# Transposing queries and keys by DMA instead of on TensorE, in a windowed attention fused with a gated feed-forward layer

## The chip, the cores and the metric

One core of a Trainium2 chip runs the whole program. The metric is device time in microseconds (us) from one launch; lower is better. Shown are the median of three runs and one profiled execution, from which all durations come.

## What is computed

Eight heads of attention over four sequences, each with 768 positions and head dimension 64. A query sees the first 8 keys and the last 96; a bias falls with the distance. The result, 3072 rows of 512, goes through a feed-forward layer that multiplies a relu branch with a linear one.

```python
scores = scale * np.matmul(q, k.transpose(0, 1, 3, 2))
is_global = pos[None, :] < int(n_global)          # n_global = 8
is_local = (rel >= 0) & (rel < int(n_local))      # n_local = 96
scores = scores + bias[None, :, :, :]             # bias = -slope * distance
scores = np.where(keep, scores, -1000000000.0)
a = np.exp(scores - np.max(scores, axis=-1, keepdims=True))
a = a / (np.sum(a, axis=-1, keepdims=True) + 1e-09)
x = (a @ v), laid out as (4 * 768, 8 * 64)
out = (np.maximum(x @ w_gate, 0.0) * (x @ w_val)) @ w_out   # 512 -> 1536 -> 512
```

Inputs and output are float32; the matmuls run in bf16 with float32 sums.

## The kernel before

The work is cut into eight halves: half s is the first or second 384 positions of sequence s // 2, with all heads. Position 3p + n of a half lies on partition p, so a half's queries are three blocks of 128, numbered n. Heads go in four pairs p.

Attention of one half, for each pair (`attention_pieces`):

- `piece_cast` (C, GpSimd from half 1 on): casts queries and keys of two heads to bf16 (L224).
- `piece_t` (T): six TensorE transposes of 128 x 128 into one PSUM tile `tp` (L235). VectorE copies the two heads' queries into a zero-padded tile `qp` (L240, L241), so that one matmul gives the scores of both. ScalarE (L252 or L259) and VectorE (two copies) put the keys into `kT` in the order of positions: seven tiles j of 8 global and 120 other keys. The second half of a sequence fills up tile 3 and writes tiles 4 to 6.
- `piece_qk` (QK, three groups): scores (L276), exponential on ScalarE (L279), times a mask in bf16 on VectorE (L288). Two PSUM buffers.
- `piece_av` (AV, one per head): values times weights (L304). The values carry columns of ones, so the sums come along; ScalarE takes their logarithm (`lnd`, L313) and the exponential of its negative (`rcp`, L318), and VectorE scales into `xT` (L321). Two PSUM buffers.

The feed-forward layer of half c (`ffn_pieces`) is 12 pairs of a gate piece (L346, relu on ScalarE L349) and a value piece (L356, product on VectorE L358), then six output pieces; each second one is copied by ScalarE (`osb`, L370) and stored by SP (L371).

Each engine works in the order in which the code issues its instructions (`manual_schedule`); semaphores hold it where an input is missing. `weave` sets that order: it issues feed-forward pieces, and between them the attention items, spread evenly by the pieces' weights. From c = 2 on, pass c weaves the layer of half c with the attention of half c+1. Before that the last eight gate/value pieces of halves 0 and 1 and both output layers are woven with the attention of half 2. SP issues the loads of q and k (`load_qk`), the spreading of global values and the stores; GpSimd issues the loads of v and of the weights.

## Time and profile before

| | |
|---|---|
| runs | 305.38, 305.5, 304.17 us; median 305.38 |
| profiled execution | 305.4 us, span 303.3 us |
| mean granted TensorE clock | 0.954 |
| TensorE matmuls busy | 254.7 us, 84% of the span |
| ScalarE, VectorE, GpSimd busy | 170.0, 163.9, 70.0 us |
| transposes (L235) | 192 matmuls, 17.2 us busy |
| GpSimd casts (L224) | 59, 30.4 us busy |
| bytes moved by DMA | 27.51 MB |

Busy times of matmuls overlap, since they are pipelined; what a matmul costs TensorE is read from one start to the next. The span is from the first to the last instruction. In rows of the profile PE is TensorE, DVE VectorE, ACT ScalarE, POOL GpSimd, SP SyncE; a bracket at a row's end gives the idle time before it and what ended it.

### The profile page before, as it was taken

How to read it: one execution, taken by the hardware profiler on the slowest of the kernel's cores; microseconds unless marked ns; L12 is line 12 of the kernel's file. 1: busy time of each engine (PE TensorE's matmuls, PEld its weight loads, DVE VectorE, ACT ScalarE, POOL GpSimd, SP SyncE). 2: the span in 40 equal slices, each digit the busy share in tenths (PEclk: the TensorE clock that was granted, in tenths of full speed). 3: DMA queues.
4: the chain of work that ended last, by engine and by line, in shares of the span. 5: the costliest groups of instructions: out<-in, count | busy, mean ns of one | idle time of the engine just before them, and what ended most of it. 6: DMA issues, size and time to landing. Idle time of an engine off the chain costs nothing.

```text
span 303.3 us, 4823 instructions
## 1 busy us (share of the span) xinstructions
PE 254.7 (84%) x1680; PEld 149.7 (49%) x1680; DVE 163.9 (54%) x458; ACT 170.0 (56%) x357; POOL 70.0 (23%) x134
## 2 busy tenths in 40 slices
PE   1264787549999889989998989999998899899994
PEld 0132345324555445655565546554664466545551
DVE  7655346552446545764476637763567457643420
ACT  8356326462345674767465755676576647664321
POOL 8960159200812400340226000400030000000000
PEclk9997589776999999999999999999999999999999
DMA  7999955908970724442862418001700110001002
GB/s 194 178 200 198 223 168 35 72 2 236 211 50 1 104 89 147 129 28 43 110 202 13 56 60 240 0 2 71 241 4 0 69 37 1 2 35 70 2 6 98
DMA packets 52400, 27.51 MB, mean 91 GB/s; under 512 B 28120, under 2 KB 49112, under 8 KB 52376
## 3 DMA queue, kind: packets, MB, share of 16 engines
q0 software_dynamic: 31856, 7.91, 26.2%
q1 hardware_dynamic: 20520, 19.30, 20.7%
q8 instruction: 13, 0.21, 0.3%
q14 instruction: 11, 0.09, 0.1%
HBM read 28.38 MB, written 6.29 MB: 114 GB/s over the span
## 4 chain that ended last, share of the span: by engine, by line
PE 68%; ACT 14%; DVE 14%; issue 2%; ACTq 0%
PE ff_ps L356 19%; PE ff_ps L346 19%; PE ff_ps L365 18%; DVE xT L321 6%; PE av_ps L304 5%; PE qk_ps L276 5%; ACT lnd L313 4%; ACT rcp L318 3%; ACT es L279 2%; PE tp L235 2%; DVE qp L241 2%; ACT grelu L349 2%; ACT kT L252 1%; DVE qp L240 1%; DVE ht L358 1%
## 5 line engine op out<-in xcount | busy, mean ns | idle before, releaser
L346 PE MATMUL ff_ps<-xT,wg 128*128 128x384 bf16 x384 | 82.3, 338 | 6.1 <-DVE ht L358 3.4
L356 PE MATMUL ff_ps<-xT,wv 128*128 128x384 bf16 x384 | 81.6, 337 | 2.6 <-ACT grelu L349 2.6
L358 DVE TENSOR_TENSOR ht<-ff_ps,grelu 128x384 bf16<-128x384 f32 x96 | 53.0, 554 | 40.1 <-PE ff_ps L356 36.5
L349 ACT ACTIVATE grelu<-ff_ps 128x384 bf16<-128x384 f32 x96 | 47.4, 493 | 39.4 <-DVE ht L358 22.8
L365 PE MATMUL ff_ps<-wo_sb,ht 128*128 128x512 bf16 x288 | 68.1, 379 | 0.0
L321 DVE TENSOR_TENSOR xT<-av_ps,rcp 64x384 bf16<-64x384 f32 x64 | 35.5, 555 | 46.1 <-ACT rcp L318 38.9
L279 ACT ACTIVATE es<-qk_ps 128x432 bf16<-128x432 f32 (+2 forms) x96 | 48.8, 537 | 8.8 <-PE qk_ps L276 8.1
L356 PEld LDWEIGHTS <-wv 128*128 128x128 bf16 x384 | 37.4, 100 | 31.0 <-issue 11.7
L346 PEld LDWEIGHTS <-wg 128*128 128x128 bf16 x384 | 37.4, 101 | 28.6 <-issue 8.0
L288 DVE TENSOR_TENSOR es<-es,m_all 128x432 bf16<-128x432 bf16 (+6 forms) x144 | 41.2, 320 | 18.8 <-ACT es L279 17.6
L276 PE MATMUL qk_ps<-qp,kT 128*128 128x432 bf16 (+6 forms) x144 | 33.3, 305 | 18.7 <-ACT es L279 9.1
L224 POOL CAST qk<-qs 128x384 bf16<-128x384 f32 x28 | 14.3, 511 | 131.3 <-DMA qs<-in_q_dram 96.5
L365 PEld LDWEIGHTS <-ht 128*128 128x128 bf16 x288 | 27.0, 97 | 26.9
L313 ACT ACTIVATE lnd<-av_ps 64x384 f32<-64x384 f32 x64 | 31.1, 486 | 14.2 <-PE av_ps L304 12.5
L304 PE MATMUL av_ps<-es,vbuf 128*128 128x216 bf16 (+5 forms) x288 | 29.6, 239 | 9.7 <-DVE xT L321 9.2
L304 PEld LDWEIGHTS <-vbuf 128*128 128x128 bf16 x288 | 24.2, 104 | 25.3 <-issue 16.9
L128 POOL DMA_DIRECT2D vbuf<-in_v_dram x28 | 24.4, 876 | 11.2 <-PE av_ps L304 11.2
L276 PEld LDWEIGHTS <-kT 128*128 128x128 bf16 x144 | 14.1, 101 | 25.6 <-issue 10.2
L370 ACT COPY osb<-ff_ps 128x512 f32<-128x512 f32 x24 | 14.1, 587 | 20.7 <-PE ff_ps L365 20.4
L235 PE MATMUL tp<-ident,qk 128*128 128x128 bf16 x192 | 17.2, 230 | 7.5 <-DVE qk L224 6.1
L235 PEld LDWEIGHTS <-qk 128*128 128x128 bf16 x192 | 13.7, 103 | 11.7 <-DVE qk L224 6.1
L224 POOL CAST qk<-ks 128x384 bf16<-128x384 f32 x31 | 16.1, 522 | 14.4 <-DMA ks<-in_k_dram 14.4
(50 smaller groups left out, 102.0 us busy)
## 6 DMA issues: line engine op xcount, KB each, us to landing
out_dram<-osb SPq DMA_DIRECT2D x24, 256.0 KB, 2.0
qs<-in_q_dram SPq DMA_DIRECT2D x6, 768.0 KB, 5.9
ks<-in_k_dram SPq DMA_DIRECT2D x6, 768.0 KB, 8.1
vbuf<-in_v_dram POOLq DMA_DIRECT2D x24, 120.0 KB, 4.4
qs<-in_q_dram SPq DMA_DIRECT2D x8, 192.0 KB, 9.2
ks<-in_k_dram SPq DMA_DIRECT2D x8, 192.0 KB, 4.5
wg<-in_moe_w_gate_dram POOLq DMA_DIRECT2D x3, 512.0 KB, 8.1
wv<-in_moe_w_val_dram POOLq DMA_DIRECT2D x3, 512.0 KB, 9.9
```

Of the source, the lines that this page charges most:

```text
L235: nc.tensor.matmul(tp[:, i, n * 128 : (n + 1) * 128], lhsT=qk[:, i, n], rhs=ident, is_transpose=True, start=(i == 0 and n == 0), stop=(i = ...
L276: nc.tensor.matmul(ps[:, c : c + n_], lhsT=kt[:, j, :], rhs=qd[:, :, :, a : a + w], start=True, stop=True)
L279: nc.scalar.activation(es[:, 0:cols], ps[:, 0:cols], AF.Exp, bias=0.0, scale=scale)
L288: nc.vector.tensor_mul(e4, e4, mk)
L304: nc.tensor.matmul(av3[:, :, a : a + w], lhsT=vb[:, j, z0 : z0 + 128], rhs=es[:, c : c + NN * w].rearrange("k (n p) -> k n p", n=NN), star ...
L313: nc.scalar.activation(ln[o0 : o0 + 64], av[d0 : d0 + 64, 0:QH], AF.Ln, bias=0.0, scale=1.0)
L321: nc.vector.tensor_tensor(xT_of[s][r, p, :], av_of[s, p, e_][r, 0:QH], rc[r], op=ALU.mult)
L346: nc.tensor.matmul(psg[:, 0:QH], lhsT=w_of(wg, dc, fc), rhs=xT[:, dc, :], start=(dc == 0), stop=(dc == N_DC - 1))
L349: nc.scalar.activation(gr, psg[:, 0:QH], AF.Relu, bias=0.0, scale=1.0)
L356: nc.tensor.matmul(psv[:, 0:QH], lhsT=w_of(wv, dc, fc), rhs=xT[:, dc, :], start=(dc == 0), stop=(dc == N_DC - 1))
L358: nc.vector.tensor_tensor(ht[:, fc, :], psv[:, 0:QH], st["gr"], op=ALU.mult)
L365: nc.tensor.matmul(ps2, lhsT=ht[:, fc, n * 128 : (n + 1) * 128], rhs=wo_sb[:, fc, :], start=(fc == 0), stop=(fc == N_FC - 1))
```

## The change

Halves 0 and 1 are as before. From half 2 on TensorE transposes nothing. GpSimd casts queries to `qz`, where each head's 64 columns stand in a block of 128 whose other half is zero, and keys to `kc`. SP issues six DMA transposes per half: for each n, eight blocks of 128 x 128 from `qz` to `qT`, and four from `kc` to `kN`. The transposed zeros give the padding of `qT`. GpSimd then copies keys from `kN` into `kT` in the order of positions. These early pieces of half c+2 are woven into pass c behind the first nine attention items, a half ahead of use. For halves 2 and 3 they stand elsewhere: half 2's between the last gate/value pieces of halves 0 and 1, half 3's behind the attention of half 2, which is now woven with the output pieces alone. To make room, six pools lose a buffer.

```diff
-    stage = ctx.enter_context(tc.tile_pool(name="stage", bufs=3))
-    cast_pool = ctx.enter_context(tc.tile_pool(name="cast", bufs=4))
-    es_pool = ctx.enter_context(tc.tile_pool(name="es", bufs=4))
-    rc_pool = ctx.enter_context(tc.tile_pool(name="rc", bufs=3))
+    stage = ctx.enter_context(tc.tile_pool(name="stage", bufs=2))
+    cast_pool = ctx.enter_context(tc.tile_pool(name="cast", bufs=3))
+    es_pool = ctx.enter_context(tc.tile_pool(name="es", bufs=3))
+    rc_pool = ctx.enter_context(tc.tile_pool(name="rc", bufs=2))
...
-    osb_pool = ctx.enter_context(tc.tile_pool(name="osb", bufs=3))
+    osb_pool = ctx.enter_context(tc.tile_pool(name="osb", bufs=2))
...
-    qp = [const.tile([128, 2, QH], BF16, name=f"qp{i}") for i in range(4)]
+    qTb = [const.tile([128, HP, 2, QH], BF16, name=f"qT{i}") for i in range(2)]
+    kNb = [const.tile([128, HP, QH], BF16, name=f"kN{i}") for i in range(2)]
+    qz = [const.tile([128, NN, HP, 2, 128], BF16, name=f"qz{i}") for i in range(2)]
+    kc = [const.tile([128, NN, DM], BF16, name=f"kc{i}") for i in range(2)]
...
+    def put_keys(copy, copy_small, kt, src, half):
...
+        if half == 0:
+            copy(*put(0, 3, 0, NG, 128))
+            copy_small(*put(3, 4, 120, NG, NG + 24))
+            copy_small(kt[:, :, 0:NG], kt[:, 0:1, NG : 2 * NG].to_broadcast([128, NT, NG]))
+        else:
+            copy(*put(4, 6, 32, NG, 128))
+            copy_small(*put(3, 4, 0, NG + 24, 128))
+            copy_small(*put(6, 7, 112, NG, NG + 48))
...
+    def piece_cast_all(s, p):
+
+        qsrc = qs_of[s][:, 2 * p : 2 * p + 2, :].rearrange("t e (n d) -> t e n d", n=NN)
+        for e in range(2):
+            nc.gpsimd.tensor_copy(qz[s % 2][:, :, p, e, 64 * e : 64 * e + 64], qsrc[:, e])
+        nc.gpsimd.tensor_copy(
+            kc[s % 2].rearrange("t n (h d) -> t h n d", d=D)[:, 2 * p : 2 * p + 2],
+            ks_of[s][:, 2 * p : 2 * p + 2, :].rearrange("t e (n d) -> t e n d", n=NN))
+
+    def piece_x(s, n):
+        nc.sync.dma_start_transpose(
+            out=qTb[s % 2].rearrange("d p e t -> d (p e) t")[:, :, n * 128 : (n + 1) * 128],
+            in_=qz[s % 2][:, n].rearrange("t p e z -> t (p e z)"))
+        nc.sync.dma_start_transpose(
+            out=kNb[s % 2][:, :, n * 128 : (n + 1) * 128], in_=kc[s % 2][:, n])
+
+    def piece_order(s, p):
+        b, half = divmod(s, 2)
+        put_keys(nc.gpsimd.tensor_copy, nc.gpsimd.tensor_copy, kT[b % 2][p], kNb[s % 2][:, p], half)
+
+    def early_pieces(s):
+        out = [(0.0, lambda p=p: piece_cast_all(s, p)) for p in range(HP)]
+        out += [(0.0, lambda n=n: piece_x(s, n)) for n in range(NN)]
+        out += [(0.0, lambda p=p: piece_order(s, p)) for p in range(HP)]
+        return out
...
+        if s >= 2:
+            return QK(0) + QK(1) + AV(0) + QK(2) + AV(1) + QK(3) + AV(2) + AV(3)
...
-    weave(f1_0[2 * G2 :] + f1_1[2 * G2 :] + f2_0 + f2_1, attention_pieces(2), 0.2)
+    weave(f1_0[2 * G2 :] + f1_1[2 * G2 :], early_pieces(2))
+    weave(f2_0 + f2_1, attention_pieces(2) + early_pieces(3))
 
     for c in range(2, NHALF):
+        early = []
         if c + 2 < NHALF:
             load_qk(c + 2, 0, H)
             load_v_half(c + 2)
+            early = early_pieces(c + 2)
         f1, f2 = ffn_pieces(c)
-        weave(f1 + f2, attention_pieces(c + 1) if c + 1 < NHALF else [])
+        a_ = attention_pieces(c + 1) if c + 1 < NHALF else []
+        items = []
+        for i in range(max(len(a_), len(early))):
+            items += a_[i : i + 1]
+            if i >= 8:
+                items += early[i - 8 : i - 7]
+        items += early[max(0, len(a_) - 8):] if len(early) > len(a_) - 8 else []
+        weave(f1 + f2, items)
```

Three places show what stands where on an engine. On VectorE before, in pass 3 (attention of half 4), from the scaling of pair 0's result to the second mask of pair 2; `qp3` and `kT0_3` are the query and key tiles of pair 3:

```order
L321 TENSOR_TENSOR xT_1915<-av_ps_1895,rcp_1916 64x384
L321 TENSOR_TENSOR xT_1915<-av_ps_1909,rcp_1916 64x384
L358 TENSOR_TENSOR ht_1708<-ff_ps_1920,grelu_1907 128x384
L240 COPY qp3_114<-tp_1926 64x384
L241 COPY qp3_114<-tp_1926 64x384
L254 COPY kT0_3_106<-tp_1926 128x24
L255 COPY kT0_3_106<-kT0_3_106 128x7x8
L358 TENSOR_TENSOR ht_1708<-ff_ps_1945,grelu_1943 128x384
L288 TENSOR_TENSOR es0_1952<-es0_1952,m_all_122 128x432
L288 TENSOR_TENSOR es1_1964<-es1_1964,m_all_122 128x432
```

And now, on VectorE in the same pass, from the scaling of pair 0's result past the second mask of pair 2:

```order
L348 TENSOR_TENSOR xT_1792<-av_ps_1773,rcp_1793 64x384
L348 TENSOR_TENSOR xT_1792<-av_ps_1786,rcp_1793 64x384
L315 TENSOR_TENSOR es0_1805<-es0_1805,m_all_126 128x432
L387 TENSOR_TENSOR ht_1692<-ff_ps_1809,grelu_1802 128x384
L315 TENSOR_TENSOR es1_1826<-es1_1826,m_all_126 128x432
L387 TENSOR_TENSOR ht_1692<-ff_ps_1830,grelu_1823 128x384
L387 TENSOR_TENSOR ht_1692<-ff_ps_1846,grelu_1841 128x384
```

The four copies are gone, and feed-forward products stand between the masks of one pair. On SP before, from the loads of half 3 to those of half 4, six stores follow one another:

```order
L107 DMA qs_869<-in_q_dram 128x8x192
L107 DMA ks_870<-in_k_dram 128x8x192
L371 DMA out_0_dram<-osb_1058 128x512
L371 DMA out_0_dram<-osb_1098 128x512
L371 DMA out_0_dram<-osb_1147 128x512
L371 DMA out_0_dram<-osb_1192 128x512
L371 DMA out_0_dram<-osb_1237 128x512
L371 DMA out_0_dram<-osb_1270 128x512
L107 DMA qs_1273<-in_q_dram 128x8x192
L107 DMA ks_1274<-in_k_dram 128x8x192
```

Now, on SP from the third of these stores to the loads of half 4 (`qT1`, `kN1`, `qz1`, `kc1` are half 3's tiles):

```order
L400 DMA out_0_dram<-osb_1160 128x512
L400 DMA out_0_dram<-osb_1222 128x512
L276 DMA_TRANSPOSE qT1_112<-qz1_116 128x8x128
L279 DMA_TRANSPOSE kN1_114<-kc1_118 128x4x128
L276 DMA_TRANSPOSE qT1_112<-qz1_116 128x8x128
L279 DMA_TRANSPOSE kN1_114<-kc1_118 128x4x128
L400 DMA out_0_dram<-osb_1254 128x512
L276 DMA_TRANSPOSE qT1_112<-qz1_116 128x8x128
L279 DMA_TRANSPOSE kN1_114<-kc1_118 128x4x128
L400 DMA out_0_dram<-osb_1284 128x512
L110 DMA qs_1287<-in_q_dram 128x8x192
L110 DMA ks_1288<-in_k_dram 128x8x192
```

Half 3's transposes stand behind the fourth store, its last two behind the fifth. On GpSimd now, from the last casts of half 2 to the first of half 3, the key copies stand between and wait for the transposes:

```order
L270 CAST qz0_115<-qs_767 128x3x64 x2
L271 CAST kc0_117<-ks_768 128x2x3x64
L242 COPY kT1_0_107<-kN0_113 128x3x120
L243 COPY kT1_0_107<-kN0_113 128x24
L244 COPY kT1_0_107<-kT1_0_107 128x7x8
L242 COPY kT1_1_108<-kN0_113 128x3x120
L243 COPY kT1_1_108<-kN0_113 128x24
L244 COPY kT1_1_108<-kT1_1_108 128x7x8
```

Before, casts of the next half and value loads followed casts there, with no copies between.

More of the change, by code (lines that the diff above doesn't have):

```diff
@@ L204 @@
         nc.vector.memset(kT[0][p][:, 3, 32:128], 0.0)
-    for i in range(2):
-        nc.scalar.copy(qp[i][64:128, 0, :], zeros[64:128])
-        nc.scalar.copy(qp[i][0:64, 1, :], zeros[0:64])
+    for p in range(2):
+        nc.scalar.copy(qTb[0][64:128, p, 0, :], zeros[64:128])
+        nc.scalar.copy(qTb[0][0:64, p, 1, :], zeros[0:64])
     for h in range(H):
@@ L250, in piece_t @@
[L250 to L263 removed]
+        put_keys(nc.scalar.copy, nc.vector.tensor_copy, kt, tp[:, 1, :], half)
@@ L395, in weave, with zero_q @@
             f()
+    def zero_q(i, p):
+        nc.gpsimd.memset(qTb[i][64:128, p, 0, :].bitcast(mybir.dt.uint32), 0)
+        nc.gpsimd.memset(qTb[i][0:64, p, 1, :].bitcast(mybir.dt.uint32), 0)
     a0 = attention_pieces(0)
@@ L420 @@
     load_v_half(1)
+    for p in range(HP):
+        zero_q(1, p)
     load_w_group(2)
@@ L433 @@
         fill(nc.gpsimd, 1, j)
+    for i in range(2):
+        nc.gpsimd.memset(qz[i].rearrange("t n p e z -> t (n p e z)").bitcast(mybir.dt.uint32), 0)
     load_qk_after(2)
```

36 lines of the change are left out of this document (10 added, 26 removed).

## The prediction

> **What bounds the kernel now.** I read the head of the profile page first, then the same by stage, then TensorE in order of time through one pass, then the waits over five passes, and at the end the transfers.
>
> The page, from which the span, the engines' busy time and one group (ScalarE's copy ahead of a store) are taken:
>
> ```profile
> span 303.3 us, 4823 instructions
> PE 254.7 (84%) x1680; PEld 149.7 (49%) x1680; DVE 163.9 (54%) x458; ACT 170.0 (56%) x357; POOL 70.0 (23%) x134
> L370 ACT COPY osb<-ff_ps 128x512 f32<-128x512 f32 x24 | 14.1, 587 | 20.7 <-PE ff_ps L365 20.4
> ```
>
> TensorE is the only engine near its limit. By stage (stretch, length, busy time of PE, PEld, DVE, ACT and POOL):
>
> ```profile
> 81.10:116.10 35.00, 32.35 (x210) 18.11 (x209) 18.18 (x49) 19.59 (x42) 9.14 (x15) 1.00 0.47 63
> 116.10:148.20 32.10, 30.21 (x217) 18.24 (x216) 19.69 (x56) 20.49 (x43) 7.93 (x13) 1.00 0.40 87
> 148.20:179.90 31.70, 29.57 (x205) 17.68 (x204) 18.77 (x52) 19.94 (x43) 6.32 (x11) 1.00 0.49 91
> 243.70:275.80 32.10, 30.21 (x218) 18.29 (x217) 19.43 (x56) 20.46 (x43) 0.00 (x0) 1.00 0.07 26
> ```
>
> The first row is the stage that I call B: the last third of the first two gate/value layers and both output layers, woven with the attention of half 2. The others are the passes c = 2, 3 and 6; 4 and 5 lie between and look the same. In a pass the gate/value layer and the output layer of half c are woven with the attention of half c+1. TensorE is busy in some 30 of 32 us, VectorE and ScalarE in 20. Pass 3 in order of time (start, busy, and idle time ahead in brackets; a busy time runs about 0.16 past the start of the next row, so costs are taken from start to start):
>
> ```profile
> 150.16 0.50 PE L235 MATMUL tp<-ident,qk 128*128 128x128 bf16 x6
> 150.50 0.81 PE L356 MATMUL ff_ps<-xT,wv 128*128 128x384 bf16 x4
> 151.15 0.81 PE L346 MATMUL ff_ps<-xT,wg 128*128 128x384 bf16 x4
> ...
> 154.09 0.35 PE L276 MATMUL qk_ps<-qp,kT 128*128 128x432 bf16 x1
> 154.27 0.81 PE L346 MATMUL ff_ps<-xT,wg 128*128 128x384 bf16 x4
> ...
> 160.65 0.42 PE L304 MATMUL av_ps<-es,vbuf 128*128 128x216 bf16 x4
> 160.92 0.81 PE L346 MATMUL ff_ps<-xT,wg 128*128 128x384 bf16 x4
> ...
> 165.19 0.81 PE L346 MATMUL ff_ps<-xT,wg 128*128 128x384 bf16 x4 [0.72 <-DVE ht L358]
> 165.84 0.35 PE L276 MATMUL qk_ps<-qp,kT 128*128 128x432 bf16 x1
> 166.78 0.81 PE L356 MATMUL ff_ps<-xT,wv 128*128 128x384 bf16 x4 [0.59 <-ACT grelu L349]
> ...
> 172.52 1.46 PE L365 MATMUL ff_ps<-wo_sb,ht 128*128 128x512 bf16 x6
> 173.81 0.69 PE L304 MATMUL av_ps<-es,vbuf 128*128 128x216 bf16 x8
> 174.36 1.46 PE L365 MATMUL ff_ps<-wo_sb,ht 128*128 128x512 bf16 x6
> 176.46 0.42 PE L304 MATMUL av_ps<-es,vbuf 128*128 128x216 bf16 x4 [0.64 <-DVE xT L321]
> 177.06 0.43 PE L304 MATMUL av_ps<-es,vbuf 128*128 128x216 bf16 x4 [0.17 <-DVE xT L321]
> ```
>
> So a gate or value piece costs 0.65, an output piece 1.29, the six transposes of a head pair 0.34, a score group at most 0.18, a head's value product 0.27. The pass loses time twice: in a burst (0.72 + 0.59, with the 0.16 behind each 1.6), and where the last pair's value products wait for their PSUM buffers (0.64 + 0.17, so 1.1). The waits of TensorE over passes 2 to 6 show one such burst per pass (waited for, us in total, times, longest):
>
> ```profile
> PE av_ps L304 <- DVE xT L321: 3.5, 7, 0.6
> PE ff_ps L346 <- DVE ht L358: 3.4, 5, 0.7
> PE ff_ps L356 <- ACT grelu L349: 2.6, 5, 0.6
> ```
>
> And the chain of waits through the burst names what stands in it:
>
> ```profile
> 165.14 0.27 DVE qp L240
> 165.42 0.37 DVE qp L241
> 165.88 0.46 ACT kT L252
> ```
>
> These are the copies out of the transposes' PSUM tile: queries on VectorE, keys on ScalarE, ahead of the relu that TensorE waits for.
>
> **The change, part by part.**
>
> *Transposes off TensorE.* Halves 2 to 7 lose 4 x 0.34 = 1.34 each. Halves 3 to 7 lie in passes 2 to 6, half 2 in B. The copies go too; from the burst's chain that takes 0.27 + 0.37 + 0.46 = 1.1, so of 1.6 I leave 0.4. At the tail, pair 2's second value product and pair 3's first now stand one output piece apart, with pair 2's first one piece earlier. Before, 2.1 passed from the end of pair 2's products (174.36) to 176.46; now one less logarithm stands in it but one store copy, so about 2.0, less the 1.29 between: 0.7 is left of 1.1. A pass then gains 1.34 + 1.2 + 0.4 = 2.9. Pass 6 spreads 20 items instead of 31 and puts those two products next to each other: 2.0 is left of 2.7, gain 2.0.
>
> *Stage B.* Attention of half 2 moves out of the 16 gate/value pieces and is packed into the first seven of 12 output pieces. Content before: 16 x 0.65 + 12 x 1.29 + 1.34 + 2.1 (four pairs' scores, at most 0.54 each) + 2.2 = 31.5 of 35.0, so 3.5 is lost. After: three score groups in a row meet two score buffers (0.46 each for pairs 0 and 1), pair 2's first value product waits 0.8, and the last three products stand together, 2.1 + 0.4: 4.2. So -1.34 + 0.7 = -0.6.
>
> *Casts and key order on GpSimd.* The casts are the work of before with queries in halves; keys then need three copies per pair. The nearest price is the cast row below, 0.51 for 384 elements. 360 + 24 + 56 (even halves) or 240 + 96 + 48 elements then cost 0.5 to 1.3 per pair, the upper end for short runs; I take 1.3 and 1.1. With casts that is about 9 to 10 us of a 29 us pass, on an engine that is idle for most of it. VectorE's mask products read SBUF beside it: their sums over 20 instructions, with GpSimd busy for 7.93 us and for none:
>
> ```profile
> 116.00:148.00 32.00, 5.64 (x20) 1.00 0.39 87
> 244.00:276.00 32.00, 5.25 (x20) 1.00 0.07 26
> ```
>
> 0.4 for 8 us of GpSimd; up to 0.5 more now, on an engine with 10 us to spare: nothing, or 0.5 a pass if all fell into a burst. The Trainium skill ("SBUF — State Buffer", Who interferes with whom) has a VectorE instruction with two SBUF inputs and a GpSimd one that reads SBUF exclude each other outright. The trace agrees in sign; by that rule the sum would move by no more than those 0.5.
>
> *The crossbar block: six transfers per half, 1.18 MB, behind one another on SP.* No row of before shows one; call the block's time T. Rows for 60 to 90 us (packets, MB, share of 16 engines x 30 us), the page's row for the same queue, and a store's landing:
>
> ```profile
> q1 hardware_dynamic: 4216, 3.25, 41.1%
> q0 software_dynamic: 4304, 0.50, 26.7%
> ...
> q0 software_dynamic: 31856, 7.91, 26.2%
> ...
> out_dram<-osb SPq DMA_DIRECT2D x24, 256.0 KB, 2.0
> ```
>
> Below: SP's loads moved 3.25 MB in 0.411 x 30 us, 264 GB/s, so T = 4.5. Above: 256-byte pieces. A half has 36 blocks of 128 rows of 256 bytes, 4608 pieces; q0's cost 0.267 x 480 / 4304 = 29.8 ns of one engine there and 39.9 over the run, so T = 8.6 or 11.5. I take 8.6: the pieces are of that size, and these ran beside other transfers. 1.5 more to the last landing (a store's 2.0 less its data).
>
> Where is it waited for? GpSimd's casts of half 2 in stage B, and of keys in pass 4 (start, busy, idle before):
>
> ```profile
> 73.55 0.50 POOL L224 CAST qk<-qs 128x384 bf16<-128x384 f32 x1 [18.75 <-DMA qs<-in_q_dram]
> 76.59 0.51 POOL L224 CAST qk<-ks 128x384 bf16<-128x384 f32 x1 [2.53 <-DMA ks<-in_k_dram]
> ...
> 189.66 0.51 POOL L224 CAST qk<-ks 128x384 bf16<-128x384 f32 x1 [2.70 <-DMA ks<-in_k_dram]
> ```
>
> In passes 3 to 6 it is covered: keys land 9.8 into pass 4 (it starts at 179.9), casts end near 13.4, transfers at 13.4 + 8.6 + 1.5 = 23.5, the first pair's keys at 24.8, and the next pass asks at 29.65. That cover ends at T = 13.4. In B casts end near 80.3, transfers 90.4, keys 91.7; scores are due at 81.1 + 10.4 + 1.3 = 92.8: just covered. Behind the key copies on GpSimd stand the value loads of the next half, which nobody needs for a pass.
>
> *Half 3 is not.* Its transposes stand on SP behind the fourth store of B, and the last two behind the fifth. The fourth store needs output piece 8 and the 0.59 copy. From the end of piece 8 to the first pair's keys: 0.7 + T + 0.3 (fifth store) + 1.5 + 1.1 = T + 3.6 = 12.2. TensorE has four output pieces and one gate piece left, 5.8. It then stands still for T - 2.25 = 6.35, with the whole of pass 2 behind the score matmul. After such pauses the clock is low (chain of waits):
>
> ```profile
> 34.98 1.28 PE ff_ps L356 x4
> ...
> 38.82 1.28 PE ff_ps L346 x4
> ...
> 41.41 0.65 PE ff_ps L356 x4
> ```
>
> Four pieces at 1.28 instead of 0.65, and part of a fifth: 2.8. By the Trainium skill ("TensorE: Matmul & The Clock Gate", Part 1) the clock is halved after an idle window of about 3.4 us and comes back after as long a busy one; the trace's four slow pieces last 5.1. Pass 2: -2.9 + 6.35 + 2.8 = +6.25.
>
> *The rest.* Clearing the padded query tiles is new GpSimd work before 73 us, where that engine idles 18.75 us for data. Fewer buffers: loads reuse tiles read long before, score and reciprocal tiles are freed one pair earlier than needed, and a third store waits 2.0 for the first, which is 2.6 x 2 ago. Nothing, unless SP is late, which the half-3 term holds.
>
> **Sum**, against the profiled execution's own 305.4 (span 303.3 and 2.1 around it; the median of the runs is 305.38, the same): B -0.6, pass 2 +6.25, passes 3 to 5 -8.7, pass 6 -2.0: -5.05, so 300.3. With T = 4.5 it is -0.6 - 2.9 + 2.25 - 8.7 - 2.0 = -12, 293.4. With T = 11.5 half 2 is 1.8 late and half 3 9.25: -0.35, 305.0.
>
> **Rivals.**
> 1. *Crossbar at copy speed* (T = 4.5): half 3 costs 2.25 and no slow clock, 293.4. For it: q1's row is the same queue; against it: its packets are 770 bytes, not 256. The Trainium skill ("DMA: Bandwidth & Descriptors", Latency and other measured facts) gives transposes 261 GB/s, an estimated 4.5 us for 1.18 MB; no run here shows it yet.
> 2. *SP's transposes become the bound* (slower). From T = 11.7 the gains are eaten, from 13.4 every pass waits for its keys. With twice the dear row, T = 23: half 2 late by 13.3, pass 2 by 20.75 + 2.8, passes 3 to 6 by 9.5 each against their gains: some 366. For it: nothing bounds a crossbar transfer in the trace; against it: the DMA engines are less than half busy in B and in passes 2 and 3 (0.47, 0.40, 0.49 in their rows). The Trainium skill ("VectorE: DVE Perf Modes", The three transpose paths) gives 1309 ns for a 128 x 128 block by DMA, and advises TensorE where PSUM will do; 36 blocks one after another would be an estimated 47 us. The blocks here go four or eight to a transfer.
> 3. *A wash*: T near 11, or passes that keep their burst with GpSimd's copies in place of VectorE's; 304 to 307.
>
> **Numbers.** Forecast (T from 6 to 10.5) 0.58, own range 296 to 304; rival 1 0.16; rival 2 0.13; rival 3 0.13. A measurement here tells about 0.5% (1.5 us) from no change. Faster 0.70, same 0.11, slower 0.19. The range 292 to 309 runs from rival 1, with a pass or so gaining more, to T = 13.4 (half 2 late by 3.7, half 3 by 11.15: +3.4), and leaves out rival 2.
>
> **What would show it.** Transposes of TensorE only for halves 0 and 1 (48 of 192). Passes 3 to 5 near 28.9. One long wait of TensorE's score matmul for GpSimd at the start of pass 2, and slow pieces behind it. SP's transposes of a half lasting T, between 4.5 and 11.5. If passes 3 to 6 begin with such a wait, rival 2 holds; if pass 2 does not, rival 1. It would be wrong if the casts or copies on GpSimd take much more than 1.3 per pair, or if the burst stays.

## The result, and the profile after

The changed kernel took 296.03 us (median of four runs, 294.92 to 296.76), the kernel before, on the same chip, 304.77 (302.91 to 305.5): 0.972 of the time, 95% interval 0.966 to 0.978. Ratios are taken over executions outside a slower state of the chip, so they can differ by 0.003 from a quotient of medians. The profiled execution took 296.74, its span is 295.0. Its page begins:

```profile
span 295.0 us, 4547 instructions
PE 247.5 (84%) x1536; PEld 142.5 (48%) x1536; DVE 142.3 (48%) x362; ACT 162.9 (55%) x333; POOL 97.7 (33%) x240
```

TensorE has 144 matmuls fewer: 48 of the 192 transposes are left. VectorE lost 21.6 us of work and GpSimd gained 27.7. By stage (stretch, length, busy time of PE, PEld, DVE, ACT, POOL, clock, share of the DMA engines, GB/s): B, then passes 2 to 6.

```profile
78.99:113.43 34.44, 31.14 (x186) 16.84 (x184) 14.39 (x33) 17.67 (x38) 8.06 (x24) 1.00 0.33 79
113.43:150.52 37.09, 30.65 (x193) 17.46 (x192) 16.54 (x40) 19.63 (x39) 17.42 (x44) 0.91 0.91 147
150.52:179.56 29.04, 28.16 (x181) 16.39 (x180) 15.80 (x37) 18.88 (x39) 11.56 (x29) 1.00 0.57 130
179.56:208.72 29.16, 28.44 (x194) 16.97 (x193) 16.09 (x41) 19.52 (x39) 8.21 (x26) 1.00 0.73 140
208.72:237.31 28.59, 27.84 (x182) 16.32 (x180) 15.52 (x37) 18.88 (x39) 9.39 (x27) 1.00 0.65 135
237.31:267.63 30.32, 28.52 (x194) 16.93 (x192) 15.46 (x41) 19.41 (x39) 0.00 (x0) 1.00 0.07 27
```

Beside the kernel before, from one first gate piece to the next, both profiled executions:

| stretch | before | after | change | forecast |
|---|---|---|---|---|
| up to the first gate piece behind half 1's attention | 65.86 | 63.81 | -2.05 | 0 |
| from there to B | 15.24 | 15.18 | -0.06 | 0 |
| B | 34.99 | 34.44 | -0.55 | -0.6 |
| pass 2 | 32.13 | 37.09 | +4.96 | +6.25 |
| passes 3 to 5 | 95.49 | 86.79 | -8.70 | -8.7 |
| pass 6 | 32.06 | 30.32 | -1.74 | -2.0 |
| pass 7, and what lies around the span | 29.63 | 29.11 | -0.52 | 0 |

The waits of TensorE in passes 3 to 5 (waited for, us in total, times, longest): the lines for `ht` and for `grelu` are gone, the tail's is left.

```profile
PE av_ps L331 <- DVE xT L348: 2.2, 3, 0.8
```

TensorE at the start of pass 2 (start, busy, idle ahead in brackets):

```profile
113.43 0.81 PE L375 MATMUL ff_ps<-xT,wg 128*128 128x384 bf16 x4
118.90 0.28 PE L303 MATMUL qk_ps<-qT,kT 128*128 128x144 bf16 x1 [4.66 <-DMA qT<-qz]
119.95 0.46 PE L303 MATMUL qk_ps<-qT,kT 128*128 128x336 bf16 x1 [0.77 <-POOL kT L246]
120.20 1.49 PE L385 MATMUL ff_ps<-xT,wv 128*128 128x384 bf16 x4
121.48 0.61 PE L303 MATMUL qk_ps<-qT,kT 128*128 128x384 bf16 x2
121.89 1.45 PE L375 MATMUL ff_ps<-xT,wg 128*128 128x384 bf16 x4
123.17 0.35 PE L303 MATMUL qk_ps<-qT,kT 128*128 128x432 bf16 x1
123.36 0.81 PE L385 MATMUL ff_ps<-xT,wv 128*128 128x384 bf16 x4
```

One wait of 4.66 for half 3's queries, 0.77 for its keys in order, and two pieces at half the clock (1.28 from start to start instead of 0.65, so 1.3 lost). SP's queue shows why, and what a block costs: first and last transposes of half 2, then half 3's behind the fourth and fifth store.

```profile
78.02 1.35 SPq L276 DMA_TRANSPOSE qT<-qz  x1
79.42 1.25 SPq L279 DMA_TRANSPOSE kN<-kc  x1
...
84.73 1.27 SPq L279 DMA_TRANSPOSE kN<-kc  x1
93.90 15.50 SPq L400 DMA_DIRECT2D out_dram<-osb  x4
109.50 1.29 SPq L276 DMA_TRANSPOSE qT<-qz  x1
...
114.86 0.52 SPq L400 DMA_DIRECT2D out_dram<-osb  x1
115.43 1.29 SPq L276 DMA_TRANSPOSE qT<-qz  x1
116.76 1.28 SPq L279 DMA_TRANSPOSE kN<-kc  x1
```

And GpSimd's first key copies of halves 2 and 3:

```profile
87.49 0.54 POOL L242 COPY kT<-kN 128x360 bf16<-128x360 bf16 x1 [9.05 <-DMA kN<-kc]
...
119.48 0.42 POOL L246 COPY kT<-kN 128x240 bf16<-128x240 bf16 x1 [23.93 <-DMA kN<-kc]
```

A block holds SP for 8.0 (78.02 to 86.0), and 9.47 pass until its keys can be copied. Half 3's was ready to go when GpSimd's casts ended near 95.5, but it began at 109.50.

### The profile page after: what moved, and what is told of

The parts are those of the page before. It is cut to its first block, busy times and chain, and to the rows that moved or that the text cites. A ratio compares the mean times of both kernels' runs of the same rounds, so it can differ in the third digit from the quotient of the medians.

```text
span 295.0 us, 4547 instructions
## 1 busy us (share of the span) xinstructions
PE 247.5 (84%) x1536; PEld 142.5 (48%) x1536; DVE 142.3 (48%) x362; ACT 162.9 (55%) x333; POOL 97.7 (33%) x240
## 4 chain that ended last, share of the span: by engine, by line
PE 69%; ACT 14%; DVE 10%; issue 2%; SPq 2%; DMA 1%; POOL 0%; ACTq 0%; DVEq 0%; POOLq 0%
PE ff_ps L385 20%; PE ff_ps L375 20%; PE ff_ps L394 17%; PE av_ps L331 6%; PE qk_ps L303 6%; ACT lnd L340 4%; DVE xT L348 4%; ACT rcp L345 3%; ACT es L306 3%; DVE es L315 2%; ACT osb L399 1%; SPq L276 1%; ACT m_all L213 1%; DVE ht L387 1%; DMA kN<-kc 1%
## 5 line engine op out<-in xcount | busy, mean ns | idle before, releaser
L315 DVE TENSOR_TENSOR es<-es,m_all 128x432 bf16<-128x432 bf16 (+6 forms) x144 | 43.1, 331 | 32.3 <-ACT es L306 31.3
L303 PE MATMUL qk_ps<-qT,kT 128*128 128x432 bf16 (+6 forms) x144 | 34.8, 309 | 21.9 <-ACT es L306 8.7
L385 PEld LDWEIGHTS <-wv 128*128 128x128 bf16 x384 | 38.1, 101 | 30.4 <-issue 9.3
L331 PE MATMUL av_ps<-es,vbuf 128*128 128x216 bf16 (+5 forms) x288 | 30.7, 242 | 11.3 <-DVE xT L348 11.2
L331 PEld LDWEIGHTS <-vbuf 128*128 128x128 bf16 x288 | 25.3, 105 | 28.0 <-issue 19.1
L270 POOL CAST qz<-qs 128x192 bf16<-128x192 f32 x48 | 16.6, 372 | 41.2 <-issue 17.5
L246 POOL COPY kT<-kN 128x240 bf16<-128x240 bf16 x12 | 5.0, 416 | 41.7 <-DMA kN<-kc 41.7
L345 ACT ACTIVATE rcp<-lnd 128x384 f32<-128x384 f32 x32 | 16.7, 523 | 1.0
L242 POOL COPY kT<-kN 128x360 bf16<-128x360 bf16 x12 | 6.4, 536 | 29.0 <-DMA kN<-kc 29.0
## 6 DMA issues: line engine op xcount, KB each, us to landing
ks<-in_k_dram SPq DMA_DIRECT2D x6, 768.0 KB, 10.1
```

The costliest lines, as they stand in the source:

```text
L303: nc.tensor.matmul(ps[:, c : c + n_], lhsT=kt[:, j, :], rhs=qd[:, :, :, a : a + w], start=True, stop=True)
L315: nc.vector.tensor_mul(e4, e4, mk)
L331: nc.tensor.matmul(av3[:, :, a : a + w], lhsT=vb[:, j, z0 : z0 + 128], rhs=es[:, c : c + NN * w].rearrange("k (n p) -> k n p", n=NN), star ...
L345: nc.scalar.activation(rc, ln, AF.Exp, bias=0.0, scale=-1.0)
L385: nc.tensor.matmul(psv[:, 0:QH], lhsT=w_of(wv, dc, fc), rhs=xT[:, dc, :], start=(dc == 0), stop=(dc == N_DC - 1))
```

## The experiments

All twelve, with the lengths of their stages in the profiled execution. "A + B" runs from the first gate piece behind half 1's attention to pass 2. The first two rows are the two kernels compared; ratios are to the kernel before, run on the same chip as each kernel (its medians there: 304.18 to 304.77), with 95% intervals.

| kernel | median us | ratio | A + B | pass 2 | 3 | 4 | 5 | 6 |
|---|---|---|---|---|---|---|---|---|
| before | 304.77 | | 50.23 | 32.13 | 31.71 | 32.07 | 31.71 | 32.06 |
| changed | 296.03 | 0.972 (0.966 to 0.978) | 49.62 | 37.09 | 29.04 | 29.16 | 28.59 | 30.32 |
| half 3 early | 293.35 | 0.964 (0.960 to 0.968) | 54.38 | 29.21 | 28.66 | 29.19 | 28.60 | 30.32 |
| transposes doubled | 310.30 | 1.018 (1.013 to 1.023) | 49.63 | 37.10 | 30.27 | 34.04 | 33.65 | 33.03 |
| TensorE's part back | 303.50 | 0.999 (0.996 to 1.003) | 50.10 | 37.75 | 30.08 | 30.63 | 30.38 | 31.39 |
| and the copies | 326.69 | 1.073 (1.065 to 1.080) | 57.84 | 40.48 | 34.21 | 34.48 | 34.21 | 34.40 |
| TensorE's part, old places | 296.64 | 0.972 (0.968 to 0.976) | 49.13 | 38.85 | 30.08 | 30.61 | 30.08 | 30.61 |
| and the copies, old places | 304.47 | 1.000 (0.998 to 1.002) | 48.22 | 34.39 | 31.71 | 32.06 | 31.85 | 32.06 |
| three transposes of 12 | 294.17 | 0.966 (0.962 to 0.971) | 49.59 | 35.96 | 28.58 | 29.14 | 28.59 | 30.32 |
| third store buffer | 289.92 | 0.952 (0.947 to 0.956) | 51.35 | 29.75 | 28.91 | 29.10 | 28.59 | 30.32 |
| before, fewer buffers | 304.13 | 1.000 (0.997 to 1.002) | 50.14 | 32.08 | 31.70 | 32.04 | 31.69 | 32.04 |
| half 3 between stores | 286.35 | 0.941 (0.936 to 0.945) | 47.95 | 29.12 | 28.59 | 29.10 | 28.58 | 30.33 |
| third product buffer | 289.69 | 0.951 (0.946 to 0.956) | 49.02 | 36.07 | 27.67 | 28.23 | 27.67 | 28.73 |
| all | 280.43 | 0.922 (0.918 to 0.927) | 47.55 | 28.22 | 27.68 | 28.26 | 27.68 | 28.72 |

### What the gain of a pass consists of

**TensorE's part back.** The transposes of halves 2 to 7 return as work that nobody reads.

```diff
+            def X(p):
+                tp = tp_psum.tile([128, 2, QH], BF16, name="tp")
...
+                        nc.tensor.matmul(tp[:, i, n * 128 : (n + 1) * 128],
+                                         lhsT=kc[s % 2][:, n, 128 * p : 128 * p + 128],
+                                         rhs=ident, is_transpose=True,
...
+            g0 = QK(0)
+            return (ahead([0], g0[:1]) + ahead([1], g0[1:]) + ahead([2], QK(1)) + AV(0) + ahead([3], QK(2)) + AV(1)
+                    + QK(3) + AV(2) + AV(3))
```

`X(p)` is the six matmuls of pair p, and `ahead` puts them in front of the first of the items that it is given.

> The changed kernel, with TensorE's transposes of halves 2 to 7 put back as work that nobody reads: six per head pair, at the places where the kernel before had them, into the same PSUM tile; the crossbar's transposes stay and are the ones used. Theory (streaming on TensorE counts in full, 0.34 per head pair): 1.34 for each of halves 4 to 7, about 1.0 for half 2, whose stretch has idle time, and nothing for half 3, whose first ones fall into the wait for keys: +6 to +7, 302 to 303; no burst waits for ht and grelu appear. Rival (TensorE's time for them was never what the passes paid, the copies behind them were): within 1.5 of 296.0.

Measured: 303.50, a little above the expectation. Passes 3 to 6 grew by 1.04, 1.47, 1.79 and 1.07, 1.34 on average, with no burst. Streaming counts in full; that the average meets the forecast to the hundredth is chance, as single passes lie this far apart.

**And the copies.** `X` also does the copies of before, into two dead setup tiles.

```diff
+                nc.vector.tensor_copy(dq[0:64, 0, :], tp[0:64, 0, :])
+                nc.vector.tensor_copy(dq[64:128, 1, :], tp[64:128, 0, :])
+                put_keys(nc.scalar.copy, nc.vector.tensor_copy, dk, tp[:, 1, :], s % 2)
```

> As the run before it, with TensorE's transposes of halves 2 to 7 put back, and now also the copies out of PSUM that stood behind them, into scratch tiles that nobody reads: two on VectorE, one on ScalarE and the small ones on VectorE per head pair. Theory (the burst of waits in the middle of a pass comes from these copies, standing ahead of the relu and of the product with the gate): beside the +6 to +7 of the transposes alone, passes 3 to 6 show the waits for ht and grelu again, 1.2 each, and stage B some more: +11 to +13 against 296.0, 307 to 309, with passes 3 to 5 back at about 31.7. Rival (the copies hide beside other work and TensorE's streaming was the whole gain): the same time as the run with the transposes alone.

Measured: 326.69, far off: 3.0 to 4.1 per pass for the copies. In that profile ScalarE's key copy waits for VectorE's second query copy in 20 places, 17.3 in all for even halves and 17.9 for odd ones, as it did before the change (30 places, 21.4 and 21.3), but here three head pairs stand within four items. That this crowding makes the price is argued, not shown. The places were not those of before, so this tells the copies' price only for these places. The next two put them right.

**At the places of before.** Attention of halves 3 to 7 in the old order of 28 items, the early pieces riding on some of them; first without, then with the copies.

```diff
+            if s >= 3:
+                C = lambda p: [(0.0, lambda: None)]
+                T = lambda p: [(0.34, lambda: X(p))]
+                return (C(0) + C(1) + T(0) + C(2) + T(1) + C(3) + QK(0) + T(2) + QK(1) + AV(0) + T(3)
+                        + QK(2) + AV(1) + QK(3) + AV(2) + AV(3))
```

> The changed kernel; the attention of halves 3 to 7 stands in the order of the kernel before, spread over its 28 places, with TensorE's six transposes per head pair put back as work that nobody reads, and without the copies behind them; stage B is the changed kernel's. Theory (the gain per pass is a sum of three: 1.34 of streaming, 1.2 of the burst, which the copies make, and 0.4 at the tail, which the places make): passes 3 to 5 take 28.9 + 1.34 + 0.4 = 30.6, and the waits for ht and grelu stay away; some 301.5 to 303 in all. Rival (the burst came from the places, three score groups and value products of different pairs close to one another): passes 3 to 5 at 31.7 to 32.1 as before, 305 to 306.

> As the run with the transposes at the places of before, and now also with the copies behind them (two on VectorE, one on ScalarE that waits for those, two small ones on VectorE), into scratch that nobody reads. So TensorE, VectorE and ScalarE do in passes 3 to 6 what they did before, and GpSimd's casts and key copies and the crossbar's transposes come on top. Theory (the copies make the burst; GpSimd and the crossbar cost the others next to nothing): passes 3 to 6 return to 31.7 to 32.1, 306 to 308 in all with half 3's wait in pass 2. Rival (GpSimd's key copies slow VectorE and ScalarE in SBUF, and the crossbar the loads): passes 3 to 5 come out longer than before, 32.5 or more, over 309. The first trial of these copies, at other places, cost 5.2 per pass; were that the copies' own price and not the places', passes 3 to 5 would take 34.

Measured: pass 3 without the copies, then pass 3 with them, and the waits of passes 3 to 6 with them:

```profile
151.51:181.59 30.08, 29.26 (x205) 17.70 (x204) 15.87 (x36) 19.03 (x39) 12.01 (x29) 1.00 0.54 125
```

```profile
146.62:178.33 31.71, 29.59 (x205) 17.68 (x204) 19.06 (x52) 20.00 (x43) 12.10 (x29) 1.00 0.71 131
```

```profile
PE ff_ps L395 <- DVE ht L407: 2.7, 4, 0.7
PE ff_ps L405 <- ACT grelu L398: 2.1, 4, 0.6
```

With everything back, passes 3 to 6 take what they took before to 0.14 (31.71, 32.06, 31.85, 32.06), though GpSimd now works 12.10 in the pass instead of 6.32 and the DMA engines 0.71 of it instead of 0.49. So the casts, the key copies and the crossbar cost a pass nothing. The copies are worth 1.6 a pass (31.92 less 30.35 on average), the burst as a whole. The places alone are worth nothing that shows in passes 3 to 5 (30.26 on average without the copies, 30.36 at the changed kernel's places), but 0.8 in pass 6 (30.61 against 31.39). Both totals, 296.64 and 304.47, came out below the expectations of 301.5 to 303 and 306 to 308: in the old order scores begin with the seventh item of pass 2, and its two waits shrink from 4.66 and 0.77 to 0.90 and 0.82 with the copies, 1.05 and 0.84 without. (The first profile is of an execution of 302.0, the longest of four; 2.59 of it is the wait in pass 2 that the last section shows, with a slow clock behind it.)

**Fewer buffers alone.** The kernel before with the first ten lines of the change's diff: `stage`, `cast`, `es`, `rc` and `osb` lose a buffer each (five pools; the section on the change says six).

> The kernel before with one part of the change alone: the smaller buffer counts (staged loads 2 for 3, casts 3 for 4, score tiles 3 for 4, reciprocals 2 for 3, store tiles 2 for 3). Theory (fewer buffers cost nothing as long as the stores leave SP on time, as in the kernel before): within 1.5 of 304.3, passes at 31.7 to 32.1. Rival (buffers were already a limit, as the run with half 3 moved forward showed for the store tiles): a pass or stage B longer by 0.3 or more, 306 to 308.

Measured: 304.13 against 304.18, every pass within 0.1. Nothing, as long as SP is on time.

### How much cover the block has

**Transposes doubled.**

```diff
+        for _ in range(2 if s >= 4 else 1):
+            piece_x1(s, n)
```

`piece_x1` is the `piece_x` of the changed kernel.

> The changed kernel, with each transpose of halves 4 to 7 issued twice, so that the block of a half takes about 16 instead of 8.0 on the load queue. Theory (cover with an end: after the casts a pass has some 13 for the block): in passes 2 to 5 the first keys now come 8 later, that is 0.6, 1.8, 5.1 and 4.4 after the next pass asks for them, counted from the rows of the changed kernel (keys at GpSimd 142.4, 172.6, 205.1, 233.0; next passes 150.5, 179.6, 208.7, 237.3; first pair's copies 0.8). Passes 3 to 6 then begin with a wait of the score matmul for GpSimd, about 12 in sum, and with slow pieces behind the longer ones: 308 to 310. Rival (the block has far more cover than that, or the second transfer runs beside the first): no such waits, within 1.5 of 296.0. A second rival (the DMA engines are what the block contends for, so that loads and stores slow down with it): also waits for value loads and stores, over 312.

Measured: 310.30, just above the expectation. Passes 3 to 6 begin with waits; those of passes 4 and 5 that come first:

```profile
180.53 0.24 PE L307 MATMUL qk_ps<-qT,kT 128*128 128x144 bf16 x1 [1.35 <-DMA qT<-qz]
...
216.19 0.48 PE L307 MATMUL qk_ps<-qT,kT 128*128 128x432 bf16 x1 [2.97 <-POOL kT L244]
```

The four passes grew by 13.9 in all. The waits at their starts come to 7.6 (0.92, then 1.35 + 0.91, 2.97, and 0.55 + 0.91), less than the 12 that were worked out from the rows; pieces at the slow clock and shorter stops behind the waits make up the rest. The twelve transposes hold SP for 17.7 to 19.3 from the first to the end of the last, not 16. So the block is hidden at 8.0 and not at some 18: what the prediction's rival 2 describes is real, and its threshold, put at 13.4 there, lies between.

### Half 3's wait

**Half 3 early.** Casts and transposes of half 3 right behind the key copies of half 2.

```diff
-    weave(f1_0[2 * G2 :] + f1_1[2 * G2 :], early_pieces(2))
-    weave(f2_0 + f2_1, attention_pieces(2) + early_pieces(3))
+    e3_ = early_pieces(3)
+    weave(f1_0[2 * G2 :] + f1_1[2 * G2 :], early_pieces(2) + e3_[:7])
+    weave(f2_0 + f2_1, attention_pieces(2) + e3_[7:])
```

> The changed kernel, with the casts and the six transposes of half 3 moved forward: they are issued right behind the key copies of half 2, in the stretch of gate and value pieces, so that on the load queue they stand ahead of the output layers' stores; only half 3's key copies stay where they were. Theory (the wait of TensorE at the start of pass 2, 4.66 + 0.77, comes from the place of the transposes behind the fourth and fifth store, not from how long they take): half 3's casts ended at 95.5, so the block of about 8.0 lies at 95.5 to 103.5 and its keys are in order well before pass 2 asks at 113.4. Pass 2 then loses the 5.4 and 1.3 of slow clock behind it and comes to 30 to 30.5 instead of 37.1; the kernel gains 6 to 7 and takes 289 to 290. Rival (the wait is the price of the block itself, or it moves: the stores and the next loads now stand behind the block and are waited for): stage B or the passes behind grow by what pass 2 loses, and the time stays within 1.5 of 296.0.

Measured: 293.35, where 289 to 290 was expected. Pass 2 fell by 7.9, more than expected, but A + B grew by 4.8: the rival was right in that the wait moved. TensorE, ScalarE and SP in B:

```profile
107.60 0.44 PE L303 MATMUL qk_ps<-qT,kT 128*128 128x288 bf16 x2 [5.61 <-ACT es L306]
```

```profile
104.97 0.59 ACT L399 COPY osb<-ff_ps 128x512 f32<-128x512 f32 x1 [5.99 <-DMA out_dram<-osb]
```

```profile
101.19 1.27 SPq L279 DMA_TRANSPOSE kN<-kc  x1
102.57 16.77 SPq L400 DMA_DIRECT2D out_dram<-osb  x6
```

The first store of B leaves at 102.57, behind the block. The third copy finds both store buffers full and waits 5.99 for it; exponentials are queued behind the copy on ScalarE, and TensorE's scores wait for those.

**Third store buffer.** The same with `osb` back at three, and a setup tile written in place to make room.

> The run with half 3's casts and transposes moved forward, with three buffers instead of two for what the output layer stores (as the kernel before had; a setup tile is written in place to make room). There the wait had moved: the four stores of stage B stood behind the six transposes on the load queue until 102.6, the third copy out of the output layer waited 5.99 for the first store to leave its buffer, and TensorE 5.61 for the exponential queued behind that copy. Theory (that wait is one of buffers): the third copy now has a buffer of its own, and the fourth comes when the first store has just left, so 4 to 5.6 of the 5.6 go, stage B comes to 34.5 to 36, the kernel to 288 to 289.5. Rival (SP's queue itself is the limit, the wait only moves on to the fourth copy): less than 1.5 gained, 292 to 293.4.

Measured: 289.92, just above the expectation; A + B fell by 3.0 of the 4.8. The rival was right in that the wait moved on, but it moved at less than its old size. What is left is the fourth copy's wait:

```profile
105.40 0.58 ACT L399 COPY osb<-ff_ps 128x512 f32<-128x512 f32 x1 [3.48 <-DMA out_dram<-osb]
```

So the buffer that cost nothing in the kernel before is worth 3.4 once SP is late.

**Half 3 between stores.** Two store buffers again; each pair of transposes between two stores.

```diff
+    e3_, a2_ = early_pieces(3), attention_pieces(2)
+    weave(f1_0[2 * G2 :] + f1_1[2 * G2 :], early_pieces(2) + e3_[:4])
+    weave(f2_0 + f2_1, a2_[:3] + e3_[4:5] + a2_[3:7] + e3_[5:6] + a2_[7:11] + e3_[6:7] + a2_[11:] + e3_[7:])
```

> The changed kernel, with half 3's casts behind the key copies of half 2 and its three pairs of transposes each between two stores of stage B, instead of all six behind the fourth; two store buffers as in the changed kernel. Theory (both waits came from the order on SP's queue alone): a store is late by at most 2.6, keys are in order by 106 or so, 7 before pass 2 asks; stage B stays at 49.6 from the first gate piece, pass 2 falls from 37.1 to 29.2 to 29.8, 288.5 to 289.5 in all. Rival (with two store buffers any transposes among the stores are waited for): stage B grows by 2 or more, over 290.5.

Measured: 286.35. TensorE waits for no store and no transpose any more, and pass 2 takes 29.12. SP:

```profile
93.14 0.36 SPq L400 DMA_DIRECT2D out_dram<-osb  x1
94.68 1.23 SPq L276 DMA_TRANSPOSE qT<-qz  x1
...
97.32 0.53 SPq L400 DMA_DIRECT2D out_dram<-osb  x1
```

Both waits came from the order on one queue. It is 2 to 3 below the expectation, mostly because A + B fell by 1.7 as well. Of that, 0.9 is a stop of TensorE for exponentials in B (0.74, with the 0.16 behind it) that is gone: 27 items instead of 31 are spread over the output pieces, so attention of half 2 is packed less tightly. The rest of the 1.7 is not accounted for.

**Three transposes of 12 blocks.** Queries and keys of a half in one tile.

```diff
-        nc.sync.dma_start_transpose(out=qTb[...]..., in_=qz[s % 2][:, n]...)
-        nc.sync.dma_start_transpose(out=kNb[s % 2][:, :, n * 128 : (n + 1) * 128], in_=kc[s % 2][:, n])
+        nc.sync.dma_start_transpose(out=qkT[s % 2][:, :, n * 128 : (n + 1) * 128], in_=qkz[s % 2][:, n])
```

> The changed kernel, with padded queries and keys of a half in one tile, so that three transposes of 12 blocks do what six (three of 8, three of 4) did: the same bytes in half as many instructions. Theory (a transpose holds the load queue for a fixed 1.3, since 8 blocks took 1.30 and 4 blocks 1.27): the queue is held 3.9 instead of 8.0 per half, though the DMA engines' own work of the block, some 73% of 8.0, 5.8 to 6.3, may set the landing; the wait for half 3 at the start of pass 2 falls from 5.4 to between 2 and 3.5, and the rest stays: 292.5 to 294. Rival (the time goes with the blocks or bytes): each transpose takes 2.0 to 2.6, the block 6 to 8, and the time is 295 to 296, as without it.

Measured: 294.17, just above the expectation. SP, and the transfers of 78 to 86 (packets, MB, share of the 16 engines):

```profile
78.09 5.13 SPq L278 DMA_TRANSPOSE qkT<-qkz  x3
```

```profile
q1 hardware_dynamic: 5229, 1.57, 95.4%
```

SP is held for 5.13 instead of 8.0, but the keys are there after 7.6 (copied from 85.69) instead of 9.47: now the DMA engines are full, at 8 x 16 x 0.954 / 5229 = 23 ns a packet, and their work of 0.954 x 8 = 7.6 (621 packets of other transfers in it) is as long as the keys wait. (With six instructions the same queue's packets took 0.733 of the ten from 78 to 88, with gaps between the transposes.) Neither theory alone: an instruction holds SP for 1.3 whether it moves four or eight blocks, 1.7 for twelve, and once that is cut the engines bind. The wait in pass 2 fell from 5.4 to 4.2, not to between 2 and 3.5.

### The best version

**Third product buffer.** The transposes' PSUM bank is idle from half 2 on; every third head's value product goes there.

```diff
+        if s >= 2 and h % 3 == 2:
+            tp = tp_psum.tile([128, 2, QH], BF16, name="tp")
+            av = tp.rearrange("d i t -> d (i t)").bitcast(FP32)
+        else:
+            av = av_psum.tile([128, 512], FP32, name="av_ps")
```

> The changed kernel, with the PSUM bank of the transposes, which halves 2 to 7 no longer use, as a third buffer for the value products (every third head's product goes there). Theory (the tail's wait, 0.72 to 0.75 in passes 2 to 5 and 1.71 + 0.18 in pass 6 and B, is for one of two product buffers): pair 3's first product no longer waits; passes 2 to 5 gain 0.7 each, pass 6 and B 0.3 to 0.6 each, since there the second product waits in its place: 3.4 to 4, 292 to 293. Rival (the wait moves on to pair 3's second product or to the store copies on ScalarE): less than 1.5 gained.

Measured: 289.69, where 292 to 293 was expected. Passes 2 to 5 gained 0.9 to 1.4 each and pass 6 1.6, where 0.7 and 0.3 to 0.6 were expected. The tail's wait is gone, and in passes 3 to 5 TensorE no longer stops. A stop of 0.72 to 0.75 costs the 0.16 behind it too, so 0.9; the 1.4 is pass 3, which was longer in the changed kernel's profile (29.04) than in four other runs that leave it alone (28.58 to 28.91). In pass 6 the whole wait of 1.71 went, and the second product did not wait in its place.

**All:** this, the three transposes, half 3's each between two stores, and a third store buffer.

> All that the runs point to in one kernel: three transposes of 12 blocks instead of six, half 3's each between two stores, a third store buffer, and the freed PSUM bank as a third buffer for value products. Theory (the gains lie at different places and add up): 296.0, less 6.7 for pass 2's wait and its slow clock, less 3.4 to 4 at the tails: 285 to 286.5. Rival (they share a limit, stage B or the clock's recovery): over 288.

Measured: 280.43, 0.922 of the kernel before (0.918 to 0.927) and 0.947 of the changed one by the medians. That is 5 to 6 below the expectation, which was summed from the gains expected of the single runs. Their measured gains, 9.7 for half 3 between stores and 6.3 for the third product buffer, give 280.0: these two add up, and the three transposes and the third store buffer add nothing to them that shows. Passes 2, 3 and 6:

```profile
108.91:137.13 28.22, 28.22 (x193) 16.96 (x192) 15.65 (x40) 19.54 (x39) 9.67 (x27) 1.00 0.79 153
137.13:164.81 27.68, 27.68 (x181) 16.34 (x180) 15.21 (x37) 18.90 (x39) 10.96 (x30) 1.00 0.70 140
...
220.75:249.47 28.72, 28.52 (x194) 16.93 (x192) 15.58 (x41) 19.43 (x39) 0.00 (x0) 1.00 0.08 29
```

TensorE is busy for the whole of passes 2 to 5. Most of what is left of the kernel's losses lies before them: up to the first gate piece behind half 1's attention TensorE is busy for 32.6 of 61.4.

## Why the prediction was right

*Direction and the place of the loss were right, the size only in part.* 300.3 was forecast and 296.03 came, at the very bottom of the range of 296 to 304; two of the four runs lie below it. Between the profiled executions the gain is 8.7, where 5.05 was forecast. The 3.6 between the forecast and the profiled execution are three errors of one sign (2.05 at the start, 1.3 in pass 2, 0.5 at the end) less 0.3 in pass 6. Most of it, the start and the end, lies where the prediction put nothing, and with little more of it the time would have left the range.

*Passes 3 to 5*: -8.70 against -8.7. The sum is right in part by luck, since the split of the 2.9 was off. Streaming is the 1.34 of the forecast. The burst went whole, 1.6, where I left 0.4 of it; the tail kept its wait (0.72 to 0.75, before 0.64 + 0.17), where I took 0.4 off. The two mistakes cancelled. And the hundredth is chance: in four runs that leave these passes alone (half 3 early, three transposes of 12, third store buffer, half 3 between stores) they take 86.3 to 86.6, not 86.79. The waits had said it: `ht` and `grelu` stood behind the copies only. In B, too, two errors cancelled: pair 2's first value product did not wait its 0.8, while pair 1's scores waited 0.74 for 0.46 and smaller losses had no term.

*The time of the block* T: 8.6 taken, 8.0 measured, and 9.47 to the keys against 10.1. But the step went by the price of pieces on the DMA engines (29.8 ns), and what bounds the six transposes is SP, held 1.3 by each; that the two came out alike is luck. A packet cost 23 ns once SP held the queue up less. The 1.5 to the last landing met the 1.47 measured (87.49 less 86.0), but not by its working: a store's 2.0 less 256 KB at the prediction's own 264 GB/s leaves 1.0. The Trainium skill's 1309 ns for a block of 128 x 128 ("VectorE: DVE Perf Modes", The three transpose paths) agrees with the 1.3 of the trace as a price of an instruction of four or eight blocks; as a price of each block, which would have made rival 2, it does not.

*Pass 2*: +4.96 against +6.25. The wait for half 3 is where and why it was forecast, 5.4 for 6.35; most of it is for the queries from the transposes themselves, not for GpSimd as forecast. The slow clock behind it is 1.3, not 2.8: two pieces, not four. That term is mis-sized, because it was read off one earlier pause (whose rows hold 2.5, the fifth piece taking 0.66); the same pause of the same code is followed by slow stretches of different length from run to run (below). Without the wait pass 2 takes 29.12 (half 3 between stores), 3.0 less than before where 2.9 was forecast. So the late block cost 8.0 in all where 6.35 + 2.8 was forecast: 5.4, 1.3, and 1.3 in shorter losses behind them for which the prediction had no term.

*GpSimd*: 0.79 and 0.74 per pair for the key copies against 1.3 and 1.1. The copy of 360 elements in short runs took 0.54, little more than the cast of 384 in 0.51. Nobody waited for the difference but half 3 (0.4).

*Nothing for the rest*: right for the casts, the key copies and the buffers, shown by two runs. Not right for the start: -2.05 before anything that I priced, and -0.5 at the end and around the span.

*The rivals.* 1 is out: the block took 8.0, not 4.5. The Trainium skill's 261 GB/s for transposes ("DMA: Bandwidth & Descriptors", Latency and other measured facts) is not reached here: in the run with three transposes the queue moved 1.57 MB in 8.0, the block among them, 196 GB/s with the engines 95% busy. 2 did not happen, but doubling the block brought its waits: 310. 3 is out.

## What to carry to other kernels

Work taken off the engine that bounds gives its own time plus the waits that its copies made: price both, and see from the rows which copy stands ahead of whom. A transfer put on a queue is late by what stands ahead of it there, and makes late what stands behind it; spread a block of transfers between the stores rather than ahead of or behind them, and give each transfer more to carry while the instruction, not the engines, is the limit. When a stage no longer uses a PSUM bank, look at once for the next wait that a buffer would end.

## What the runs showed that was not expected

*A copy held up beside GpSimd, at a difference of 0.03 us.* The 2.05 at the start is mostly one event. VectorE and GpSimd in the kernel before:

```profile
13.37 1.90 DVE L255 COPY kT<-kT 128x56 bf16<-128x56 bf16 x1
13.45 2.02 DVE L224 CAST qk<-qs 128x384 bf16<-128x384 f32 x1
```

```profile
13.41 1.56 POOL L148 MEMSET vbuf<- 128x544 uint32 x3
```

and in the changed kernel:

```profile
13.34 0.17 DVE L244 COPY kT<-kT 128x56 bf16<-128x56 bf16 x1
13.42 0.79 DVE L227 CAST qk<-qs 128x384 bf16<-128x384 f32 x1
```

```profile
13.41 1.78 POOL L151 MEMSET vbuf<- 128x544 uint32 x3
```

The copy starts 0.04 ahead of GpSimd's memset and takes 1.90, or 0.07 ahead and takes 0.17; TensorE's wait for it is 4.02 or 2.26. Both profiles of kernels that start like the kernel before (itself and the one with fewer buffers) have the copy 0.04 ahead and long, the twelve with the changed start 0.06 or 0.07 ahead and short. That these hundredths decide is read from the rows and not tested. Which edit moved the copy was not tried either; the buffer counts alone did not. (The clock can move as much: the kernel with fewer buffers has the long copy, and yet its first gate piece behind half 1's attention comes at 63.30, before the changed kernel's at 63.81, since its slow stretches were shorter.) The same happened once in the middle of a pass, in the execution of 302.0: two mask products, of which the first started within 0.02 of the first of GpSimd's casts, took 3.89 until the last cast had begun, and TensorE waited 2.59 for the product with the gate behind them.

```profile
127.78 3.89 DVE L315 TENSOR_TENSOR es<-es,m_all 128x144 bf16<-128x144 bf16 x2 [1.01 <-ACT es L306]
```

```profile
127.76 0.64 POOL L270 CAST qz<-qs 128x192 bf16<-128x192 f32 x2
...
131.44 0.60 POOL L271 CAST kc<-ks 128x384 bf16<-128x384 f32 x1
```

The Trainium skill ("SBUF — State Buffer", Who interferes with whom) says that such pairs exclude each other and that the order of issue decides who is held up. These rows agree with the first. They do not show the second, since the copy starts ahead of the memset whether it is held up or not, and several GpSimd instructions got through before the mask products ended. The averages do not show it (mask products 320 ns before, 331 after), and the prediction's 0.5 came from sums of such products.

*The slow clock after the same pause differs from run to run.* The same code after the same wait, in the changed kernel and in the run with doubled transposes:

```profile
35.54 1.48 PE L385 MATMUL ff_ps<-xT,wv 128*128 128x384 bf16 x4
36.82 1.32 PE L375 MATMUL ff_ps<-xT,wg 128*128 128x384 bf16 x4
37.97 0.81 PE L385 MATMUL ff_ps<-xT,wv 128*128 128x384 bf16 x4
```

```profile
34.27 1.36 PE L379 MATMUL ff_ps<-xT,wg 128*128 128x384 bf16 x4
35.47 0.81 PE L389 MATMUL ff_ps<-xT,wv 128*128 128x384 bf16 x4
```

The clock is back 2.5 sooner in the second, 37.97 against 35.47. Over the twelve profiles with the changed start the first gate piece behind half 1's attention comes at 61.3 to 64.0, about the 2 to 3 us by which runs of one kernel differ here. The Trainium skill ("TensorE: Matmul & The Clock Gate", Part 1) calls the length variable from run to run, since the window that watches activity runs free; the rows agree that it varies. A term for a slow clock behind a pause can only be forecast as a range.
